# Two layers of linear attention and gated MLP: turning two more row tiles through DRAM instead of on TensorE

## The chip, the cores and the metric

The kernel runs on one core of a Trainium2 chip. A core has a matrix engine (TensorE, PE in the profile, with its weight loads as PEld), a vector engine (VectorE, DVE), a scalar engine (ScalarE, ACT), a general engine (GpSimd, POOL) and a sync engine (SyncE, SP), which here does nothing but issue DMA transfers. Each engine works through its own queue in order; they wait for each other through semaphores. SBUF is the memory on the core, PSUM the eight accumulation banks that TensorE writes, DRAM the memory off the core. The metric is the device time of one execution in microseconds, as the median of several runs.

## The reference

`x` has 2048 rows of 512 floats. Two layers follow each other with the same weights. In each, an attention block and a mixer block are added to `x`:

```python
x = x + A(layernorm(x))          # linear attention, 32 heads of 16
x = x + B(layernorm(x))          # gated MLP that mixes the rows

# A: phi(t) = where(t > 0, t + 1, exp(t)) + 1e-6
kv = einsum("bhsd,bhse->bhde", phi(k), v);  z = einsum("bhsd->bhd", phi(k))
o  = einsum("bhqd,bhde->bhqe", phi(q), kv) / (einsum("bhqd,bhd->bhq", phi(q), z) + 1e-6)
return o @ wo

# B: w_in is 512 x 1792, w_sp is 2048 x 2048
z  = gelu(x @ w_in);  z1 = z[:, :896];  z2 = layernorm(z[:, 896:])
return (z1 * (w_sp @ z2 + b_sp)) @ w_out
```

Everything is in float32 and has to stay that exact.

## The kernel before

**Numbers in two parts.** A float32 operand is split into a high part (a copy in the faster format float32r, made by ScalarE, line 224) and a low part (what is left over, made by VectorE, line 227, or by GpSimd, line 232). A product takes three matmuls: high by high, high by low, low by high (`mm3`, lines 238 to 240). So each operand of a matmul costs a ScalarE copy and a subtraction before TensorE can use it.

**Tiles and stages.** The rows are worked in 16 tiles of 128. For each layer L there are three stages. The first (`P1`) normalises the input, makes phi(q) and phi(k) and sums up k against the input. `transition` turns these sums into one 512 x 512 matrix `W2` and a vector. The second (`P2`) applies `W2` to each tile, adds the result to x, normalises to y, turns y so that features lie on the partitions, and multiplies y by `w_in`. The third (`P4`) mixes rows with `w_sp` and multiplies by `w_out`; its matmuls, lines 2076 to 2078, are most of the time.

**One step of the second stage.** `P2.run` (layer 0) and `P2.run2` (layer 1) are loops over steps s, with several tiles under way at a time. In step s:

- `c(s-1)`: twelve matmuls by `W2` into a PSUM bank; `c2` adds the bank to x (line 922) and takes the row statistics (lines 369 to 376, VectorE then GpSimd); `c3` stores x (line 928), normalises to y on ScalarE (line 382) and hands y to `Turn.store`.
- `a`, `a2` and `b`: multiply the queries of tiles s+3 and s+2 by their denominators (lines 867, 879 to 888), turn them, and split tile s for the next `c`.
- `d_high(s-2)` and `d_low(s-2)`: take up the turned y of tile s-2, with the high copy by ScalarE (line 224) and the low part by VectorE (line 227), written into a quarter of `xT`.
- `e(s-3)`: 24 matmuls of 448 columns for the half of `w_in` that is mixed later; `e2` is their gelu on ScalarE (line 1087), `e3` and `e4` the layer norm over it (line 382 again, 896 columns wide).
- `f`: twelve matmuls for the other half of `w_in`, on four tiles of y together; the first come in step 6, from when tiles 0 to 3 are in `xT`.

In layer 0, loads and adds of `w_sp` for the third stage go along in these steps (`sums.ask`, `sums.tick`; lines 1725, 1730), and pieces of `w_in` are loaded and split (`w1.piece`, `w1.fetch`). In layer 1 tiles from 4 on go through `epair` and `odd`, which the change does not touch.

**Two ways to turn a tile.** `Turn` (line 408) knows two. For a tile in its list `by_pe`, `get` runs four transposes of 128 x 128 on TensorE (line 394) into a PSUM bank. For another, `c3` normalises into another order of the columns, `store` writes the tile to DRAM by a transfer that SP issues (line 430), `load` reads it back in another layout (line 206), and `pre` turns its 32 x 32 blocks on VectorE (line 459). The turned tile goes to a PSUM bank in layer 0 for tiles below 13, and to the tile's own place in SBUF (`ZHome`) in layer 1. The queries are turned the same two ways with a list of their own: tiles 0 to 2 on TensorE, the others through DRAM (`qt`; in the DMA rows `qt<-pg` is a store and `pg<-qt` a load, and `yt` likewise for y).

**What sets the order.** All instructions are issued in the order of the program text; nothing is rescheduled. Where a DMA reads what another has written, SP waits for the landing and holds back all that it has to issue after that. In layer 0 a step asks SP for: the load of x for tile s+1; the store of x of tile s-1 and, if that tile goes through DRAM, its y store; the stores and loads of `sums.ask`; the query store of tile s+2; then, at the end of the step, the query load of tile s+2 (`qturn.load`), the y load of tile s-1 (`xturn.load`), and a piece of `w_in`. In layer 1 the query load comes at the head of the next step, so the y load of tile s-1 stands behind the query store of tile s+2.

SBUF is handed out in pages that go round (`pages`), and PSUM in eight banks likewise; whoever gets a page waits for the one who had it last.

Of the kernel before, what the change touches and what calls it, by code (L numbers as in the profile page):

```python
# [19 lines left out]
NT = S // P  # L20
# [103 lines left out]
QBANK = 13, 13  # L124
YBANK = 13
# [37 lines left out]
def mixer_kernel(ctx: ExitStack, tc: tile.TileContext, x_in, wqkv, wo_d, win1_d, win2_d, wsp_d, bsp_d, wout_d,  # L163
# [59 lines left out]
    def high(h, src):  # L223
        nc.scalar.activation(h, src, AF.Copy)  # L224

    def low(l, src, h):
        nc.vector.tensor_sub(l, src, h.bitcast(F32))  # L227

    def split(h, l, src, pool=False):
        high(h, src)  # L230
        if pool:
            nc.gpsimd.tensor_tensor(l, src, h.bitcast(F32), op=OP.subtract)
        else:
            low(l, src, h)
# [7 lines left out]
    class Weight:  # L242


        def __init__(self, slots, shape, pieces, turned=False):
            self.slots, self.shape, self.pieces, self.turned = slots, shape, pieces, turned
            self.h = self.l = None
            self.raw = deque()
            self.n_load = self.n_split = 0
# [40 lines left out]
    def w_in1():  # L290
        return Weight(bigs, [P, NF, 4, P], [win1_d[f] for f in range(NF)])
# [95 lines left out]
    def feats(ap, turned):  # L387

        return ap.rearrange("p (g c j) -> p c g j" if turned else "p (c g j) -> p c g j", g=4, c=4)
# [382 lines left out]
    def transition(p1, p2, sums):  # L772
        wv, wo = p1.wv, p1.wo
        zh, zl = pages.get(PAGE, F32R), pages.get(PAGE, F32R)
        za = p1.zacc
        nc.vector.tensor_scalar(za, za, NT * PHI_EPS, None, op0=OP.add)
        split(zh, zl, za, True)
        pages.put(za)
        p1.late()
        p1.wk.free()  # L780
        if p1.L == 0:
            sums.store2()
            sums.slots.close()
            sums.slots = pages
            sums.fetch()
        g = quads.get([P, 4, 512])
        for c in range(4):
            (high if c % 2 == 0 else nc.vector.tensor_copy)(g[:, c, :], p1.G[c])
            banks.put(p1.G[c])
        if p1.L == 0:  # L790
            sums.add2(0, 4)
        zb = banks.get(PAGE)
        nc.tensor.matmul(zb, ones, zh, start=True, stop=False)
        nc.tensor.matmul(zb, ones, zl, start=False, stop=True)
        pages.put(zh, zl)
        p2.zbc = pages.get(PAGE)
        nc.scalar.activation(feats(p2.zbc, True), feats(zb, False), AF.Copy)
        banks.put(zb)
        p2.a(0)
        p1.late_phi()  # L800
        if p2.win1 is not None:
            p2.win1.fetch()
            p2.win1.fetch()
        p2.zeps = small.tile([P, 32], F32, name="zeps", bufs=1)
        nc.vector.tensor_reduce(p2.zeps, p2.zbc.rearrange("p (h d) -> p h d", d=16), axis=mybir.AxisListType.X,
                                op=OP.add)
        nc.vector.tensor_scalar(p2.zeps, p2.zeps, PHI_EPS, PHI_EPS, op0=OP.mult, op1=OP.add)

        p2.a2_den(0)
        m = pages.get([P, 4, P])  # L810
        for q in range(4):
            b = banks.get([P, P])
            s = slice(q * P, (q + 1) * P)
            for c in range(4):
                nc.tensor.matmul(b, wv[:, c, s], g[:, c, s], start=c == 0, stop=c == 3)
            nc.vector.tensor_mul(m[:, q, :], b, mask)
            banks.put(b)
        quads.put(g, wv)
        p2.a2_mul(0)
        p2.a(1)  # L820
        p1.late()
        p2.a2_den(1)
        p2.W2 = (quads.get([P, 4, 512], F32R), quads.get([P, 4, 512], F32R))
        for q in range(4):
            b = banks.get(PAGE)
            nc.tensor.matmul(b, m[:, q, :], wo[:, q, :], start=True, stop=True)
            split(p2.W2[0][:, q, :], p2.W2[1][:, q, :], b)
            banks.put(b)
            if q == 1:
                p2.b(0)  # L830
        pages.put(m)
        quads.put(wo)
        p2.a(2)
        p1.late_phi()
        p2.a2_mul(1)
        p1.late()
        p2.a(3)
        p2.a2(2)
        p1.late_phi_a()


    class P2:
        def __init__(self, p1):
            self.L = L = p1.L
            self.p1 = p1
            self.win1, self.win2 = None if L else w_in1(), p1.win2
            self.ws = deque()
            self.wf = deque([] if not L else [w1parts[f] for f in list(range(NF)) * 2 + [0, 6, 1, 2, 6]]
                            + [w1sums[f, m] for m in range(2) for f in range(3)]
                            + [[t[:, 256:512] for t in w1parts[f + 3]] for f in range(3)])  # L850
            self.draw, self.S, self.fdone, self.qhome, self.zacc, self.meant = {}, {}, None, {}, {}, set()
            self.qturn, self.xturn = Turn(f"qt{L}", range(3), True, banked=range(QBANK[L])), Turn(f"yt{L}", (0, 1, 2, 3, NT - 1), home=ZHome, copy=bool(L), banked=() if L else range(YBANK))
            self.qp, self.qT, self.x, self.ms, self.xB, self.z, self.zms = {}, {}, {}, {}, {}, {}, {}
            self.fq = deque()
            self.fnext = []
            self.A, self.u, self.y = {}, {}, {}
# [484 lines left out]
        def run(self, sums):  # L1341
# [4 lines left out]
            for s in range(1, NT + 3):  # L1346
# [4 lines left out]
                if s < 5:  # L1351
                    self.c(s - 1)
                    self.b_high(s)
                    self.c2(s - 1)
                    self.p1.late_phi_b()
                    self.b_low(s)
                    if s >= 2:
                        self.d_high(s - 2)
                        self.d_low(s - 2)
                    self.p1.late()  # L1360
                    self.c3(s - 1)
                    sums.ask()
                    self.a2(s + 2)
                    self.p1.late_phi_a()
                    self.a(s + 3)
                    sums.tick(ask=False)
                else:
                    if s < NT:
                        self.b_high(s)
                    self.a2_den(s + 2)  # L1370
                    if s < NT:
                        self.b_low(s)
                    if s <= NT:
                        self.c(s - 1)
                        self.c2(s - 1)
                    if s == NT:
                        quads.put(*self.W2)
                        pages.put(self.zbc)
                    self.a2_mul(s + 2)
                    late = s - 2 in self.xturn.by_pe and s <= NT or AHEAD <= s <= NT  # L1380
                    if s in (NT, NT + 1):
                        self.e(s - 3)
                        self.e2(s - 3)
                    if late:
                        self.d_high(s - 2)
                        self.d_low(s - 2)
                    if s <= NT:
                        self.c3(s - 1)
                    self.a(s + 3)
                    if s <= NT + 1 and not late:  # L1390
                        self.d_high(s - 2)
                        self.d_low(s - 2)
# [106 lines left out]
        def run2(self):  # L1499
            late = self.p1  # L1500
            for s in range(1, NT + 3):
# [5 lines left out]
                if s < 5:  # L1507
# [2 lines left out]
                    self.c2(s - 1)  # L1510
                    late.late_phi_b()
                    self.b_low(s)
                    if s >= 2:
                        self.d_high(s - 2)
                        self.d_low(s - 2)
                    late.late()
# [1 line left out]
                    self.a2(s + 2)  # L1518
                    late.late_phi_a()
                    self.a(s + 3)  # L1520
                else:
                    def b():
                        if s < NT:
                            self.b_high(s)
# [1000 lines left out]
    p1 = P1(0)  # L2525
    p1.start()
    for L in range(2):
        p1.run(sums)
        p2 = P2(p1)
        p2.loadx(0)  # L2530
        p2.loadx(1)
        transition(p1, p2, sums)
        if L == 0:

            sums.store2()
            sums.tick()
        p2.p4 = p4 = P4(p2, sums)
        p2.run(sums)
        nxt = P1(1) if L == 0 else None
        p4.run(nxt)  # L2540
        p1 = nxt
# [31 lines left out]
```

## Time and profile before

| | |
|---|---|
| median of three runs | 1335.68 us (1335.37 to 1336.0) |
| the profiled execution | 1337.64 us, of which the span of its instructions is 1335.8 us |
| instructions | 19338, of them 6493 matmuls |
| TensorE clock granted | 1.00 over the span |
| data moved by DMA | 312.86 MB |
| line 793 of the transition starts, layer 0 and layer 1 | 129.70 us, 800.30 us |
| from the start of `e(0)` to the end of `e(3)`, layer 0 and layer 1 | 158.48 to 187.23 us, 829.56 to 858.31 us |

A row of a group reads: line, engine, operation, written tile <- read tiles, partitions x elements, count, then busy time and mean length. A row of the timeline reads: start in us, length in us, engine, line, operation, tiles, count, and in brackets how long the engine stood idle before it and what ended that. Matmuls overlap, so the time that a matmul takes from its neighbours is the distance between two starts and not its length. SPq rows are the issue of a transfer, not the transfer.

### The profile page before, as it was taken

How to read it: one execution, taken by the hardware profiler on the slowest of the kernel's cores; microseconds unless marked ns; L12 is line 12 of the kernel's file. 1: busy time of each engine (PE TensorE's matmuls, PEld its weight loads, DVE VectorE, ACT ScalarE, POOL GpSimd, SP SyncE). 2: the span in 40 equal slices, each digit the busy share in tenths (PEclk: the TensorE clock that was granted, in tenths of full speed). 3: DMA queues.
4: the chain of work that ended last, by engine and by line, in shares of the span. 5: the costliest groups of instructions: out<-in, count | busy, mean ns of one | idle time of the engine just before them, and what ended most of it. 6: DMA issues, size and time to landing. Idle time of an engine off the chain costs nothing.

```text
span 1335.8 us, 19338 instructions
## 1 busy us (share of the span) xinstructions
PE 1329.5 (100%) x6493; PEld 1132.0 (85%) x6493; DVE 1075.2 (80%) x1731; ACT 755.0 (57%) x1275; POOL 485.9 (36%) x632
## 2 busy tenths in 40 slices
PE   9999999999999999999999999999999999999998
PEld 7888888888888888889988878888888888888898
DVE  7679965768897889898867878678789988899885
ACT  5674543347743264445667755557588643666464
POOL 3765765533037400301424554554532022122021
PEclk9999999999999999999999999999999999999999
DMA  5898588987989896895987883678777876579344
GB/s 185 272 316 274 192 271 288 306 276 244 313 304 359 258 269 203 288 332 165 201 187 222 230 219 87 208 246 261 231 223 241 254 248 197 176 245 319 114 79 65
DMA packets 182532, 312.86 MB, mean 234 GB/s; under 512 B 15392, under 2 KB 56352, under 8 KB 182048
## 3 DMA queue, kind: packets, MB, share of 16 engines
q1 hardware_dynamic: 160672, 265.60, 59.6%
q0 software_dynamic: 21616, 45.88, 15.9%
q8 instruction: 51, 0.84, 0.3%
q14 instruction: 49, 0.40, 0.1%
q10 hardware_dynamic: 144, 0.13, 0.0%
HBM read 223.22 MB, written 113.51 MB: 252 GB/s over the span
## 4 chain that ended last, share of the span: by engine, by line
PE 87%; DVE 4%; DMA 4%; ACT 2%; POOL 2%; SPq 1%; issue 1%; POOLq 0%; DVEq 0%; ACTq 0%
PE bank L2076 12%; PE bank L2077 12%; PE bank L2078 12%; PE bank L240 10%; PE bank L238 10%; PE bank L239 10%; PE bank L2277 3%; PE bank L2278 3%; PE bank L2279 3%; PE bank L1173 1%; PE bank L1174 1%; PE bank L1172 1%; PE bank L1001 1%; PE bank L1003 1%; PE bank L1002 1%
## 5 line engine op out<-in xcount | busy, mean ns | idle before, releaser
L2076 PE MATMUL bank<-qd,pg 128*128 128x512 f32 x708 | 275.4, 389 | 0.0
L2077 PE MATMUL bank<-qd,pg 128*128 128x512 f32 x708 | 275.4, 389 | 0.0
L2078 PE MATMUL bank<-qd,pg 128*128 128x512 f32 x708 | 275.4, 389 | 0.0
L1829 ACT ACTIVATE qd<-qd 128x1024 fp32r<-128x1024 f32 x148 | 155.9, 1054 | 96.8 <-PE bank L2078 67.6
L1832 DVE TENSOR_TENSOR qd<-qd,qd 128x1024 fp32r<-128x1024 f32 x133 | 169.1, 1272 | 25.6 <-ACT qd L1829 25.4
L240 PE MATMUL bank<-qd,pg 128*128 128x512 f32 x448 | 174.8, 390 | 0.0
L2078 PEld LDWEIGHTS bank<-qd,pg 128*128 128x128 f32 x708 | 132.9, 188 | 27.7
L2076 PEld LDWEIGHTS bank<-qd,pg 128*128 128x128 f32 x708 | 132.9, 188 | 27.5
L2077 PEld LDWEIGHTS bank<-qd,pg 128*128 128x128 f32 x708 | 132.9, 188 | 27.3
L238 PE MATMUL bank<-qd,pg 128*128 128x512 f32 x264 | 103.2, 391 | 0.6 <-DVE pg L227 0.4
L239 PE MATMUL bank<-qd,pg 128*128 128x512 f32 x264 | 103.0, 390 | 0.0
L240 PEld LDWEIGHTS bank<-qd,pg 128*128 128x128 f32 x448 | 84.1, 188 | 18.4 <-DVE pg L227 0.9
L1730 POOL TENSOR_TENSOR pg<-pg,pg 128x512 f32<-128x512 f32 x48 | 71.9, 1498 | 64.7 <-DMA pg<-in_wsp_dram 60.4
L2117 POOL TENSOR_TENSOR bg<-bg,pg 128x512 f32<-128x512 f32 x28 | 52.1, 1863 | 115.4 <-ACT qd L1829 115.4
L373 POOL TENSOR_SCALAR rs<-mv 128x1 f32<-128x1 f32 x76 | 24.0, 315 | 165.8 <-DVE mv L371 159.7
L224 ACT ACTIVATE pg<-pg 128x512 fp32r<-128x512 f32 (+1 forms) x94 | 55.2, 597 | 51.0 <-DVE pg L1935 20.3
L2279 PE MATMUL bank<-wo,qd 128*128 128x256 f32 x288 | 81.5, 283 | 0.0
L2277 PE MATMUL bank<-wo,qd 128*128 128x256 f32 x276 | 78.1, 283 | 0.0
L2278 PE MATMUL bank<-wo,qd 128*128 128x256 f32 x276 | 78.0, 283 | 0.0
L227 DVE TENSOR_TENSOR pg<-pg,pg 128x512 fp32r<-128x512 f32 (+1 forms) x92 | 59.7, 657 | 5.7 <-ACT pg L224 5.4
L459 DVE STREAM_TRANSPOSE bank<-pg 128x512 f32<-128x512 f32 x58 | 41.6, 717 | 26.7 <-DMA pg<-yt 16.4
L238 PE MATMUL bank<-bg,qd 128*128 128x448 f32 x160 | 59.3, 371 | 0.1
(306 smaller groups left out, 3407.0 us busy)
## 6 DMA issues: line engine op xcount, KB each, us to landing
qd<-s SPq DMA_DIRECT2D x62, 512.0 KB, 5.0
qd<-hP SPq DMA_DIRECT2D x48, 512.0 KB, 5.0
qd<-in_wsp_dram SPq DMA_DIRECT2D x43, 512.0 KB, 4.9
pg<-z SPq DMA_DIRECT2D x56, 256.0 KB, 5.5
pg<-in_wsp_dram SPq DMA_DIRECT2D x52, 256.0 KB, 4.8
s<-pg SPq DMA_DIRECT2D x48, 256.0 KB, 4.3
z<-pg SPq DMA_DIRECT2D x40, 256.0 KB, 3.6
pg<-w POOLq DMA_DIRECT2D x38, 256.0 KB, 5.3
```

The source lines that it names most:

```text
L238: nc.tensor.matmul(out, ah, bh, start=start, stop=False)
L239: nc.tensor.matmul(out, ah, bl, start=False, stop=False)
L240: nc.tensor.matmul(out, al, bh, start=False, stop=stop)
L1730: nc.gpsimd.tensor_tensor(t, a, b, op=OP.add)
L1829: self.mark = nc.scalar.activation(w[:, 0], r, AF.Copy)
L1832: nc.vector.tensor_sub(w[:, 1], r, w[:, 0].bitcast(F32))
L2076: m(out, h[:, o], w[:, 0, j, :], start=start, stop=False, skip_group_check=True)
L2077: m(out, h[:, o], w[:, 1, j, :], start=False, stop=False, skip_group_check=True)
L2078: m(out, l[:, o], w[:, 0, j, :], start=False, stop=stop, skip_group_check=True)
L2277: m(out, A, x, start=start and f == 0, stop=False, skip_group_check=True)
L2278: m(out, A, y, start=False, stop=False, skip_group_check=True)
L2279: m(out, B, x, start=False, stop=stop and f == 2, skip_group_check=True)
```

## The change

Three places change.

1. In `transition`, the low part of the sum of phi(k) (`zl`) is made by GpSimd in layer 0, as it was, and by VectorE in layer 1. In VectorE's queue it stands ahead of the copies of `G` (line 788), in TensorE's it is read by line 794.
2. `xturn`'s list `by_pe` loses tiles 2 and 3, in both layers. These two tiles of y are now normalised into the other order, stored, loaded and turned on VectorE, like tiles 4 to 14.
3. In the first steps, `d` of tile s-2 stood behind `b_low` and ahead of `c3`. For tiles 0 and 1 it stays there. For tile 2 it moves to the end of step 4, behind `c3`, `a2`, `a` and, in layer 0, `sums.tick`. For tile 3, in step 5, no line moves, but the list decides there too: a tile that is not in `by_pe` is taken up behind `c3` instead of ahead of it (`late` in layer 0, `ahead` in layer 1).

```diff
@@ transition
-        split(zh, zl, za, True)
+        split(zh, zl, za, p1.L == 0)
@@ P2.__init__
-            ... self.xturn = Turn(f"yt{L}", (0, 1, 2, 3, NT - 1), home=ZHome, copy=bool(L), banked=() if L else range(YBANK))
+            ... self.xturn = Turn(f"yt{L}", (0, 1, NT - 1), home=ZHome, copy=bool(L), banked=() if L else range(YBANK))
@@ P2.run, steps 1 to 4
-                    if s >= 2:
+                    if 2 <= s < 4:
                         self.d_high(s - 2)
                         self.d_low(s - 2)
                     self.p1.late()
...
                     self.a(s + 3)
                     sums.tick(ask=False)
+                    if s == 4:
+                        self.d_high(2)
+                        self.d_low(2)
@@ P2.run2, steps 1 to 4
-                    if s >= 2:
+                    if 2 <= s < 4:
                         self.d_high(s - 2)
                         self.d_low(s - 2)
                     late.late()
...
                     self.a(s + 3)
+                    if s == 4:
+                        self.d_high(2)
+                        self.d_low(2)
```

More of the change, by code (lines that the diff above doesn't have):

```diff
@@ L851, in __init__ @@
             self.draw, self.S, self.fdone, self.qhome, self.zacc, self.meant = {}, {}, None, {}, {}, set()
-            self.qturn, self.xturn = Turn(f"qt{L}", range(3), True, banked=range(QBANK[L])), Turn(f"yt{L}", (0, 1, 2, 3, NT - 1), home=ZHome, copy=bool(L), banked=() if L else range(YBANK))
+            self.qturn, self.xturn = Turn(f"qt{L}", range(3), True, banked=range(QBANK[L])), Turn(f"yt{L}", (0, 1, NT - 1), home=ZHome, copy=bool(L), banked=() if L else range(YBANK))
             self.qp, self.qT, self.x, self.ms, self.xB, self.z, self.zms = {}, {}, {}, {}, {}, {}, {}
```

## The prediction

> **What bounds the kernel now.** I read the page first, then what TensorE (PE) waited for, then the timeline of each engine around the two stretches where tiles 2 and 3 of y are handled, layer 0 at 163 to 189 us and layer 1 at 834 to 859 us.
>
> ```profile
> span 1335.8 us, 19338 instructions
> ...
> PE 1329.5 (100%) x6493; PEld 1132.0 (85%) x6493; DVE 1075.2 (80%) x1731; ACT 755.0 (57%) x1275; POOL 485.9 (36%) x632
> ```
>
> ```profile
> PE bank L623 <- DVE ones_f L189: 1.0, 1, 1.0
> ```
>
> PE is busy in 1329.5 of 1335.8 us, and its longest single wait is 1.0 us, at the very start. So PE's issue order is the time: whatever leaves PE is gained in full, and whatever PE has to wait for in the new order is lost in full, since no later gap gives it back. The sum is made against the profiled execution (1337.64 us, its span 1335.8 and 1.8 around it); the timed median is 1335.68, 1.96 lower, and I carry the difference that I work out over to the median.
>
> **The change part by part.** I write d(i) for taking up tile i of y (turn, high copy on ScalarE, low part on VectorE), e(i) for its gate matmuls, which need d(i), and c(i) for the projection that makes tile i.
>
> *What PE loses.* Here is d(2) in layer 0, the turn between c(3) and e(1):
>
> ```profile
> 166.28 0.60 PE L394 MATMUL bank<-ident,pg 128*128 128x128 f32 x4
> ...
> 166.92 0.37 PE L239 MATMUL bank<-bg,qd 128*128 128x448 f32 x1
> 167.12 0.36 PE L240 MATMUL bank<-bg,qd 128*128 128x448 f32 x1
> ```
>
> From the first transpose to the second matmul of e(1) it is 0.64 us; one matmul of e takes a slot of 0.20 (167.12 - 166.92), so four transposes hold PE for 0.44. Two tiles in two layers: 4 x 0.44 = 1.76 us gone. The row shows why length misleads: 0.60 for four that overlap. [...] The trace has slots of 0.11, and I use those.
>
> *What comes instead in layer 0.* The tile is normalised in the other layout (L382, 0.82 us for either), stored, loaded back and turned on VectorE. The stores and loads go through SP's queue, in program order. Step 3 issues: x store of tile 2 (L928), then, new, the y store of tile 2; sums and spatial-weight transfers; the q store of tile 5 (L430); at the step's end the q load of tile 5, and right behind it, new, the y load of tile 2.
>
> ```profile
> 163.95 0.38 SPq L928 DMA_DIRECT2D x<-pg  x1
> ...
> 168.17 0.41 SPq L430 DMA_DIRECT2D qt<-pg  x1
> 172.87 0.33 SPq L206 DMA_DIRECT2D pg<-qt  x1
> 173.25 0.42 SPq L206 DMA_DIRECT2D pg<-in_win_dram  x1
> ...
> 176.54 1.22 SPq L430 DMA_DIRECT2D qt<-pg  x1
> 181.50 0.32 SPq L206 DMA_DIRECT2D pg<-qt  x1
> ```
>
> The q load stands at the head of the queue from 168.6 until its own store has landed, 172.87. The y load of tile 2 can't pass it: it is issued where L206's win load is now, 173.25, and later by what the new y store takes in front of it. The seven transfers from the x store of 163.95 to the q store were through at 172.87, so one costs at most 1.3; I take half of that, 0.65, and 173.9 for the issue.
>
> ```profile
>   DVE bank L459: 16.4, 9
> ...
> DMA to landing us min/median/max: 2.6/3.3/6.6
> ```
>
> That is the answer for the y transfers of layer 0: the loads of later tiles land 2.6 us after issue at best, 3.3 in the middle, and VectorE has already waited 16.4 us for nine of them. I take 2.9, between the first two, since the queue has just been waited out: landed at 176.8. Bounds: 173.25 + 2.6 = 175.9 and 174.5 + 6.6 = 181.1.
>
> ```profile
> 171.58 0.39 PE L238 MATMUL bank<-qd,pg 128*128 128x512 f32 x1
> ...
> 174.32 0.60 PE L394 MATMUL bank<-ident,pg 128*128 128x128 f32 x4
> ...
> 179.62 0.40 PE L238 MATMUL bank<-qd,z_q 128*128 128x512 f32 x1
> ```
>
> ```profile
> 172.65 1.33 DVE L888 SCALAR_TENSOR_TENSOR pg<-z_q,den 128x512 f32<-128x512 f32 x1
> ...
> 176.54 0.69 DVE L459 STREAM_TRANSPOSE bank<-pg 128x512 f32<-128x512 f32 x1
> ...
> 178.55 0.69 DVE L227 TENSOR_TENSOR pg<-bank,z_q 128x512 fp32r<-128x512 f32 x1 [0.16 <-DMA x<-pg]
> ...
> 181.27 0.69 DVE L227 TENSOR_TENSOR qd<-bank,qd 128x512 fp32r<-128x512 f32 x1
> ```
>
> ```profile
> 162.68 0.82 ACT L382 ACTIVATE pg<-pg,nb,rs 128x512 f32<-128x512 f32 x1 [1.69 <-POOL nb L376]
> ...
> 173.65 1.12 ACT L382 ACTIVATE z_z<-z_z,nb,rs 128x896 f32<-128x896 f32 x1
> ...
> 177.26 0.60 ACT L224 ACTIVATE z_q<-bank 128x512 fp32r<-128x512 f32 x1 [1.12 <-DVE bank L459]
> ...
> 182.49 0.82 ACT L382 ACTIVATE pg<-pg,nb,rs 128x512 f32<-128x512 f32 x1 [4.14 <-POOL nb L376]
> ```
>
> First wait, e(2). VectorE's step 4 ends with L888 (172.65 + 1.33 = 174.0); then, new, d(2) sits there until 176.8. Turn 0.69, high copy 0.60, low part 0.69: the high part is there at 178.2, the low part at 178.9. e(2)'s third matmul is the first to read the low part, two slots of 0.20 behind its first, so e(2) starts as if at 178.5. PE gets there when c(4) is done: 174.32 less the transposes of d(2) = 173.9. The wait is 4.6 us (3.7 with the early bound, 8.9 with the late one).
>
> Second wait, e(3). ScalarE's queue holds the high copy of d(2) ahead of e(0)'s normalise (now 173.65) and e(1)'s two gelus, so these start at about 178.1 and the b part of tile 5 follows as it does now: turn 2.9 after that normalise (176.54 - 173.65), low part 2.0 after the turn (178.55), so 182.9 to 183.6. c(5) is reached at 178.5 + 4.86 = 183.4 (e is 174.76 to 179.62 now): no wait. The normalise of tile 4 comes 3.9 after that low part starts (182.49 - 178.55), at 186.8; d(3) is no longer ahead of it but behind it, so its high copy is done at about 188.2 and its low part at 188.9; the y load of tile 3, behind the q load of 181.50 (and 2.0 later for three new transfers of 0.65), is issued at 183.8, lands near 186.7 and is turned by 187.4, just in time. e(3) starts as if at 188.5; PE has done c(5) (2.74 long) at 186.1. Wait 2.4 (1.3 if the normalise is not late, 3.5 with one slow transfer). In step 6, e(3) and two f tiles (twelve matmuls each, as c) give VectorE and ScalarE 4.86 + 2 x 2.74 = 10.3 us to catch up, and nothing of this is passed on.
>
> Layer 0: +4.6 + 2.4 - 0.88 = **+6.1 us**.
>
> *Layer 1.* Here the q load is issued a step later in the order and the y load of tile 2 stands right behind the q store of tile 5:
>
> ```profile
> 835.17 0.37 SPq L430 DMA_DIRECT2D qt<-pg  x1
> ...
> 839.00 0.32 SPq L206 DMA_DIRECT2D pg<-qt  x1
> ```
>
> ```profile
> 841.61 1.69 DVE L888 SCALAR_TENSOR_TENSOR pg<-z_q,den 128x512 f32<-128x512 f32 x1
> ...
> 846.47 0.69 DVE L227 TENSOR_TENSOR pg<-bank,z_q 128x512 fp32r<-128x512 f32 x1 [1.35 <-ACT z_q L224]
> ...
> 858.05 1.09 DVE L459 STREAM_TRANSPOSE z_y<-pg 128x512 f32<-128x512 f32 x1
> ```
>
> ```profile
> 842.25 1.12 ACT L382 ACTIVATE z_z<-z_z,acc 128x896 f32<-128x896 f32 x1
> ...
> 850.40 0.82 ACT L382 ACTIVATE pg<-pg,nb,rs 128x512 f32<-128x512 f32 x1 [3.48 <-POOL nb L376]
> ```
>
> ```profile
> 850.71 0.40 PE L238 MATMUL bank<-qd,z_q 128*128 128x512 f32 x1
> ...
> 853.45 0.36 PE L238 MATMUL bank<-bg,qd 128*128 128x448 f32 x1
> ```
>
> The y store stands ahead of 835.17 and the load waits for it some 3 to 4 us (the q store took 3.8), so it lands by about 842. VectorE frees at 842.7 (L888's end less the 0.6 of the low part that is gone from before it), or near 841.7 if L888 doesn't take 1.69 there. The turn into SBUF is 1.09, the high copy 0.60: e(0)'s normalise (842.25) moves to between 843.4 and 844.4, by 1.1 to 2.1. e(2), at 850.71 - 4.86 - 0.88 = 845.0, has its low part at 845.1 at the latest, before its third matmul. The b part of tile 5 (846.47) moves to 848.6 at most, c(5) is at 849.8: covered. The normalise of tile 4 (850.40) moves to 851.5 to 852.5; high copy and low part of d(3) behind it end 2.05 later, so e(3) starts as if at 853.1 to 854.2, against 853.45 - 0.88 = 852.6. Wait 0.5 to 1.6, I take 1.0. Layer 1: 1.0 - 0.88 = **+0.1**.
>
> *The low part in layer 1's transition.*
>
> ```profile
> 798.78 1.27 DVE L788 COPY qd<-bank 128x512 f32<-128x512 f32 x2
> ...
> 799.61 1.29 POOL L232 TENSOR_TENSOR pg<-pg,pg 128x512 fp32r<-128x512 f32 x1 [1.70 <-ACT pg L224]
> ...
> 800.30 0.39 PE L793 MATMUL bank<-pg,ones 128*128 128x512 f32 x1
> 800.95 0.50 PE L794 MATMUL bank<-pg,ones 128*128 128x512 f32 x1 [0.26 <-POOL pg L232]
> 801.28 1.95 PE L815 MATMUL bank<-qd,qd 128*128 128x128 f32 x16
> ```
>
> PE waits for POOL's low part: L794 could start a slot of 0.23 behind L793, at 800.53, and starts 0.4 later. On VectorE the part takes 0.69 from 799.6, so it is there at 800.3 and the 0.4 is saved. But the two G copies now stand behind it and end at 801.5 instead of 800.1, and L815, which could begin at 800.9, reads them: if each matmul needs its own quarter, the last copy is just in time; if the first one needs all four, it starts at 801.5, 0.2 later than now. Between -0.4 and +0.2; I take **-0.2**.
>
> Sum: 6.1 + 0.1 - 0.2 = **+6.0 us**, 1335.68 + 6.0 = **1341.7 us**. With the low ends (3.7 + 1.3 - 0.88, 0.5 - 0.88, -0.4) it is +3.3; with the high ends (8.9 + 3.5 - 0.88, 1.6 - 0.88, +0.2) +12.4.
>
> **The rivals.**
>
> *No wait at all.* If both tiles were back before PE needs them, only the 1.76 and the 0.4 count: 1335.68 - 2.2 = 1333.5. It speaks for it that later tiles take this way without holding PE up. Against it: their steps hold f tiles besides, while step 5 lasts 8.0 (171.58 to 179.62), and it decides only if the y load is issued by 169.3, 4.6 us earlier, ahead of the q load that holds the queue. Chance 0.05.
>
> *Only a short wait.* One of the two waits in layer 0 falls out, because the load is taken out of its turn or d(3) finds ScalarE free before the normalise: 6.0 - 4.6 = +1.4 or 6.0 - 2.4 = +3.6, so 1337.1 or 1339.3. Chance 0.12.
>
> *The clock falls as well.* A gap of 4.6 us would be several times the longest so far.
>
> ```profile
> 2.35 3.41 PE L630 MATMUL bank<-pg,ones 128*128 128x512 f32 x8
> ```
>
> At the start, after idling, PE issued eight matmuls of 512 columns in 3.41 us, 0.43 each; in c(4) twelve take 2.74, 0.23 each. If a gap brings that pace back for 3.4 us, half of it is lost: +1.7, so 1343.4. No gap in this trace is long enough to tell. [...] Chance 0.18.
>
> *More waits.* The pages go round in another order and a reused one may be held by a store (L227 at 178.55 waits 0.16 for the x store's page now); with a wait as long as the late bound of the first, 1335.68 + 12.4 = 1348.1. Chance 0.05.
>
> **How the numbers follow.** The forecast has the remaining 0.60. The range takes the low and high ends of the sum without the rarest: 1337.2 to 1346.2. It holds the forecast but for its outermost ends, the fall of the clock, and the upper half of the short-wait case. A measurement of this kernel can tell about 0.2% (2.7 us): faster would be under 1333.0, no change up to 1338.4. The no-wait case is within 0.2%, so faster has 0.03; and so is the nearer half of the short-wait case, with a little of the forecast's low end: 0.13; slower 0.84.
>
> **What would show it.** PE should show waits before the first matmuls of e(2) and e(3) in layer 0 (L238 with 448 columns) of about 4.6 and 2.4 us, released by VectorE's L227 or ScalarE's L224, and one near 1 us in layer 1. SP should issue the y load of tile 2 between 173 and 174.5, behind a q load; VectorE's L459 should wait for it from 174 on. There should be 16 fewer transposes on L394. The wait of L794 on POOL should be gone. I am wrong if that y load is issued before 170, or if e(2) in layer 0 starts within 1 us of c(4)'s end.

## The result, and the profile after

The changed kernel takes 1344.07 us (median of six runs, 1343.53 to 1348.9), the kernel before beside it 1335.84 (six runs, 1334.76 to 1338.6). The ratio is 1.0065 with a 95% interval of 1.0048 to 1.0081: slower by 6 to 11 us. Predicted was 1341.7, in a range of 1337.2 to 1346.2. Further down, a ratio is turned into microseconds by taking 1336 as the time before.

The profiled execution after took 1348.9 us (clock 0.996 over the span). The head of its page, and what TensorE waited for (line of the waiting instruction, releaser, then microseconds in total, times, the longest):

```profile
span 1347.0 us, 19318 instructions
PE 1333.0 (99%) x6477; PEld 1133.8 (84%) x6477; DVE 1074.7 (80%) x1736; ACT 754.4 (56%) x1275; POOL 484.1 (36%) x631
```

```profile
PE bank L238 <- ACT qd L224: 6.0, 2, 4.4
PE bank L238 <- ACT z_h L224: 2.8, 1, 2.8
```

There are 16 matmuls fewer, as there should be. The two waits on the high copies of `qd` are e(2) and e(3) of layer 0. The wait on `z_h` comes and goes between executions, as shown below. The row of L794 waiting on GpSimd is gone.

Now layer 0 around tiles 2 and 3. First SP's issues (start, length of the issue):

```profile
172.21 0.33 SPq L206 DMA_DIRECT2D pg<-qt  x1
172.59 0.42 SPq L206 DMA_DIRECT2D pg<-yt  x1
...
177.66 0.60 SPq L430 DMA_DIRECT2D qt<-pg  x1
182.80 0.32 SPq L206 DMA_DIRECT2D pg<-qt  x1
183.21 0.38 SPq L206 DMA_DIRECT2D pg<-yt  x1
```

Both y loads go out directly behind a q load, and each q load has waited for its own store: the one of 177.66 holds the queue until 182.80. VectorE then sits before the turn of each tile (in brackets the idle time and what ended it), and ScalarE before the high copy:

```profile
176.43 0.73 DVE L459 STREAM_TRANSPOSE bank<-pg 128x512 f32<-128x512 f32 x1 [3.05 <-DMA pg<-yt]
...
187.47 0.73 DVE L459 STREAM_TRANSPOSE bank<-pg 128x512 f32<-128x512 f32 x1 [2.38 <-DMA pg<-yt]
```

```profile
177.19 0.60 ACT L224 ACTIVATE qd<-bank 128x512 fp32r<-128x512 f32 x1 [4.12 <-DVE bank L459]
...
188.23 0.60 ACT L224 ACTIVATE qd<-bank 128x512 fp32r<-128x512 f32 x1 [1.19 <-DVE bank L459]
```

And TensorE, from the last matmul of c(4) into e(2), and from the last of c(5) into e(3):

```profile
173.08 0.39 PE L240 MATMUL bank<-qd,pg 128*128 128x512 f32 x1
177.84 0.74 PE L238 MATMUL bank<-bg,qd 128*128 128x448 f32 x1 [4.37 <-ACT qd L224]
178.38 0.57 PE L239 MATMUL bank<-bg,qd 128*128 128x448 f32 x1
178.75 0.57 PE L240 MATMUL bank<-bg,qd 128*128 128x448 f32 x1
...
180.99 0.39 PE L240 MATMUL bank<-bg,qd 128*128 128x448 f32 x1
181.22 0.37 PE L238 MATMUL bank<-bg,qd 128*128 128x448 f32 x1
...
186.85 0.39 PE L240 MATMUL bank<-qd,pg 128*128 128x512 f32 x1
188.88 0.47 PE L238 MATMUL bank<-bg,qd 128*128 128x448 f32 x1 [1.64 <-ACT qd L224]
```

Start to start, 173.08 to 177.84 is 4.76 where 0.23 would do: 4.5 us lost. But the loss does not end there. The next matmuls start 0.37 apart (178.38 to 178.75) where one of 448 columns takes 0.20: nine of them, from 177.84 to 181.22, take 3.38 us instead of 1.84, so 1.5 more are lost. TensorE came back from the gap at about half its pace: the granted clock is 0.50 from 177.63 to 181.04 and 1.00 on both sides of that. The second gap costs 1.8 us (188.88 less 186.85 less 0.23), and 0.2 more where the third matmul waits for the low part. In the kernel before there was no gap ahead of e(3):

```profile
182.14 0.39 PE L240 MATMUL bank<-qd,pg 128*128 128x512 f32 x1
182.36 0.36 PE L238 MATMUL bank<-bg,qd 128*128 128x448 f32 x1
```

Layer 1's e(3) starts 0.46 behind the last matmul of c(5), where 0.23 is a slot, and the transition no longer waits:

```profile
862.99 0.39 PE L240 MATMUL bank<-qd,pg 128*128 128x512 f32 x1
863.45 0.47 PE L238 MATMUL bank<-bg,qd 128*128 128x448 f32 x1
```

```profile
811.41 0.39 PE L793 MATMUL bank<-pg,ones 128*128 128x512 f32 x1
811.64 0.40 PE L794 MATMUL bank<-pg,ones 128*128 128x512 f32 x1
811.88 3.73 PE L815 MATMUL bank<-qd,qd 128*128 128x128 f32 x32
```

From L793 to L815 it was 0.98 before (801.28 - 800.30) and is 0.47 now.

### The profile page after: what moved, and what is told of

It reads as the page before. It is cut to its first block, busy times and chain, and to the rows that moved or that the text cites. A ratio compares the mean times of both kernels' runs of the same rounds, so it can differ in the third digit from the quotient of the medians.

```text
span 1347.0 us, 19318 instructions
## 1 busy us (share of the span) xinstructions
PE 1333.0 (99%) x6477; PEld 1133.8 (84%) x6477; DVE 1074.7 (80%) x1736; ACT 754.4 (56%) x1275; POOL 484.1 (36%) x631
## 4 chain that ended last, share of the span: by engine, by line
PE 91%; DVE 3%; DMA 2%; ACT 2%; issue 1%; POOL 1%; SPq 0%; POOLq 0%; ACTq 0%; DVEq 0%
PE bank L2083 12%; PE bank L2084 12%; PE bank L2082 12%; PE bank L240 11%; PE bank L238 11%; PE bank L239 11%; PE bank L2283 3%; PE bank L2284 3%; PE bank L2285 3%; PE bank L1174 1%; PE bank L1173 1%; PE bank L1172 1%; DMA pg<-xt 1%; PE bank L1001 1%; PE bank L1003 1%; PE bank L1002 1%
```

## The experiments

The theory: all of the loss is in layer 0 and is made of e(2)'s and e(3)'s waits for a y load that stands behind a q load on SP's queue. The rivals: layer 1 or the transition carries part of it; the order on SP's queue does not matter, because the transfer itself or VectorE's place for it is late; the clock, not the wait, is what costs.

**The change in layer 0 alone, and in layer 1 alone.** The list of tiles, the order of `d` and the transition, each by layer:

```diff
# layer 0 alone
-   Turn(f"yt{L}", (0, 1, NT - 1), ...)
+   Turn(f"yt{L}", (0, 1, 2, 3, NT - 1) if L else (0, 1, NT - 1), ...)
    run2 and transition as before the change
# layer 1 alone
+   Turn(f"yt{L}", (0, 1, 2, 3, NT - 1) if L == 0 else (0, 1, NT - 1), ...)
    run as before the change
```

> The change in layer 0 alone: tiles 2 and 3 through DRAM and tile 2 at the end of step 4 there, layer 1 and its transition as before. Theory (two waits of TensorE in layer 0, for e(2) and e(3), carry the loss, and layer 1 gains a little): 6.5 to 8 us slower than before, with waits of about 4.4 and 2 us on L238 before e(2) and e(3) and slow matmuls after the first. Rival (a good part of the loss comes with layer 1, for example the wait of 2.8 us near 786 us that the profile after shows): 5 us slower or less.

> The change in layer 1 alone, with the low part of its transition on VectorE; layer 0 as before. Theory: 8 transposes at 0.11 and the wait of L794 go (0.88 and 0.42), a wait of about 0.45 before e(3) comes, so 0.6 to 1.1 us faster than before. Rival (layer 1 carries part of the loss): 1 to 2 us slower.

Layer 0 alone: 1343.59 us, ratio 1.0053 (1.004 to 1.0066), so +7.1 us (5.3 to 8.8). Layer 1 alone: 1336.94, ratio 1.0007 (0.9996 to 1.0019), between -0.5 and +2.5. The place is layer 0. In its profile e(3), expected to wait about 2 us, waits only some 0.6 with the low part, and e(2) waits as in the changed kernel:

```profile
177.86 0.47 PE L238 MATMUL bank<-bg,qd 128*128 128x448 f32 x1 [4.18 <-ACT qd L224]
```

The gain expected of layer 1 alone is not to be seen; a gain of more than 0.5 us is excluded. Its e(3) starts 0.71 behind c(5), a wait of 0.5:

```profile
855.47 0.39 PE L240 MATMUL bank<-qd,pg 128*128 128x512 f32 x1
856.18 0.47 PE L238 MATMUL bank<-bg,qd 128*128 128x448 f32 x1 [0.33 <-ACT qd L224]
```

The profile of layer 1 alone also bears on the wait on `z_h`, of which it has its own:

```profile
PE bank L238 <- ACT z_h L224: 2.9, 1, 2.9
```

It is in layer 1's first stage, near 783 us, ahead of everything that this kernel changes, and the profiled execution of before has no wait over 0.5 us there. So it comes and goes by execution; no trace here shows it in the kernel before itself. In the profile after, this wait and the slow matmuls behind it (granted clock 0.50 from 788.61 to 795.44) take some 5.6 us; that execution lay 4.8 above its median. The changed kernel was run again:

> The changed kernel once more, on the chip of these runs. Theory: 7 to 8.5 us slower than before, with waits of 4.4 us before e(2) and 0.5 to 2 us before e(3) in layer 0 and slow matmuls behind the first; a wait of some 3 us late in layer 1's first stage, which the profile after showed and the one of before did not, comes and goes from run to run and is no part of the change. Rival: that wait is there again and makes a part of the 8 us.

It gave 1344.15 us, ratio 1.0058 (1.0045 to 1.007), and a profiled execution of 1343.89, where e(2) and e(3) of layer 0 read:

```profile
173.62 0.39 PE L240 MATMUL bank<-qd,pg 128*128 128x512 f32 x1
177.67 0.47 PE L238 MATMUL bank<-bg,qd 128*128 128x448 f32 x1 [3.66 <-ACT qd L224]
...
187.09 0.39 PE L240 MATMUL bank<-qd,pg 128*128 128x512 f32 x1
188.33 0.47 PE L238 MATMUL bank<-bg,qd 128*128 128x448 f32 x1 [0.85 <-ACT qd L224]
```

Without the `z_h` wait, this execution is 6.25 us above the profiled one of before (1343.89 - 1337.64). Its terms are taken up below.

**The y load ahead of the q load.** In steps 3 and 4 of layer 0 the two loads change places:

```diff
+               if s in (3, 4):
+                   self.xturn.load(s - 1)
                self.qturn.load(s + 2)
-               self.xturn.load(s - 1)
+               if s not in (3, 4):
+                   self.xturn.load(s - 1)
```

> As the changed kernel, but in layer 0 the y loads of tiles 2 and 3 are issued ahead of the query loads of steps 3 and 4 instead of behind them. Theory (the wait for e(2) is mostly the y load standing behind a query load that holds SP's queue until its own store has landed): the load of tile 2 is issued near 168.5 instead of 172.6, e(2) waits 1.5 to 2 us instead of 4.5, no slow matmuls follow, e(3) waits 1 to 2.5; 3 to 4 us slower than before, so 4 to 5 us faster than the changed kernel. Rival (VectorE's and ScalarE's order binds, not the queue): e(2) still waits 3.5 us or more and the time stays within 1 us of the changed kernel's.

1340.83 us, ratio 1.004 (1.0027 to 1.0054): +5.3 us, 2.4 to 3.3 less than the changed kernel by the ratios and the medians, where 4 to 5 less had been expected.

```profile
169.39 0.45 SPq L206 DMA_DIRECT2D pg<-yt  x1
174.33 0.32 SPq L206 DMA_DIRECT2D pg<-qt  x1
```

```profile
174.93 0.73 DVE L459 STREAM_TRANSPOSE bank<-pg 128x512 f32<-128x512 f32 x1 [1.58 <-DMA pg<-yt]
```

```profile
176.34 0.68 PE L238 MATMUL bank<-bg,qd 128*128 128x448 f32 x1 [2.28 <-ACT qd L224]
176.82 0.57 PE L239 MATMUL bank<-bg,qd 128*128 128x448 f32 x1
```

The queue's order is a third to a half of the first wait: with the load out 3.2 us earlier (169.39 against 172.59; 173.35 in the second profile), e(2)'s loss falls from 4.5 (3.8 in the second profile) to 2.4 (176.34 - 173.67 - 0.23, c(4)'s last matmul starting at 173.67). Half of the head start or more is eaten by the transfer, which now needs 5.5 us until VectorE has the tile (169.39 to 174.93) instead of 3.8 or 2.9. In this trace the three loads of `w_sp` and the query store issued ahead of it land at 172.22, 172.89, 173.55 and 174.31 and the y load at 174.91, in the order of their issue. So the query load's wait is not all: the four transfers ahead came through first. And two expectations fell: the matmuls behind the shorter gap are slow all the same, 0.37 apart, and e(3), expected to wait 1 to 2.5 us, starts 0.4 behind its slot (185.41 to 186.07), so that here the 1.5 us of slow matmuls are not hidden in a second wait. (This execution also has the wait on `z_h` and took 1345.16 us.)

**The gap filled with work.** Twenty matmuls of 448 columns whose result is overwritten, ahead of e(2) in layer 0:

```diff
+               if self.L == 0 and i == 2 and j == 0:
+                   for _ in range(20):
+                       nc.tensor.matmul(b, self.W2[0][:, 0, 0:P], self.W2[0][:, 0, 0:HF], start=True, stop=True)
```

> As the changed kernel, with 20 matmuls of 448 columns whose result is overwritten put in front of e(2) in layer 0; they take about 4.1 us and keep TensorE busy while it would wait. Both theories: the matmuls of e(2) keep the fast slot of 0.20 us. Theory (the slow matmuls lengthen the kernel): 1.2 to 1.6 us faster than the changed kernel. Rival (the next wait, for tile 3's load, does not move with TensorE, so e(3) starts when it did): within 0.4 us of the changed kernel, and the wait before e(3) grows from 2.0 to about 3.5 us.

1345.17 us, ratio 1.0062 (1.0048 to 1.0075): no better than the changed kernel, as the rival had it. The profiled execution took 1348.60, 3.4 above the median:

```profile
173.61 4.22 PE L1073 MATMUL bank<-qd 128*128 128x448 f32 x20
178.78 0.48 PE L238 MATMUL bank<-bg,qd 128*128 128x448 f32 x1 [0.94 <-ACT qd L224]
...
189.95 0.74 PE L238 MATMUL bank<-bg,qd 128*128 128x448 f32 x1 [2.98 <-ACT qd L224]
```

The work did keep e(2) fast, but e(3) now waits 3 us and it is there that the slow matmuls come, and they go on twice as long, from 189.95 to 196.1. Tile 3 is not back sooner because TensorE works faster: its load is issued when SP's queue gets to it (in this execution behind a q load of 184.63). So what is saved at e(2) is waited for at e(3). What the slow matmuls alone cost, this run can't tell, as it has longer ones of its own.

**One tile alone.** Tile 3 alone through DRAM in layer 0, and tile 2 alone, with everything else as before:

```diff
# tile 3 alone
+   Turn(f"yt{L}", (0, 1, 2, 3, NT - 1) if L else (0, 1, 2, NT - 1), ...)
# tile 2 alone, with its d at the end of step 4
+   Turn(f"yt{L}", (0, 1, 2, 3, NT - 1) if L else (0, 1, 3, NT - 1), ...)
```

> In layer 0 tile 3 alone goes through DRAM; tile 2 stays on TensorE in its old place, layer 1 and its transition are as before. Theory (the load of a tile is ready at a time that SP's queue sets, whatever TensorE does; in the changed kernel the first wait hides most of the second): the y load of tile 3 is issued near 182.7 behind a query load and lands near 186 to 187, e(3) would be reached at 181.9 and waits 5 to 6.5 us; 5 to 8 us slower than before, almost what both tiles cost together. Rival (each tile adds its own price, and tile 3's is the 0.6 to 2 us that e(3) waits in the changed kernel): 0 to 2 us slower.

> Layer 0 with tile 2 alone turned through DRAM and taken up at the end of step 4; tile 3, layer 1 and the transition as before. The wait before e(2) must come as in the changed kernel, 3.8 to 4.5 us, and, being longer than 3.9 us or near it, one window at half clock behind it (eight or nine matmuls of 448 columns at 0.37 instead of 0.20, 1.5 us); tile 3 is turned on TensorE, so e(3) should start without a wait of over 0.5. Theory: 4.2 + 0.2 + 1.5 less the 0.44 of the transposes, +5.5 us (4.5 to 6.5). The costs of tile 2 alone (5.5) and of tile 3 alone (measured +6.1) would then add up to 11.6, where the two together cost 6.9 to 8: they overlap. Rival (the clock costs nothing here, only the wait counts): +3.5 to +4.2. Rival (costs add up): both together minus tile 3 alone, +1 to +2.

Tile 3 alone: 1342.54 us, ratio 1.0038 (1.0025 to 1.0052), +5.1 us (3.3 to 6.9). Tile 2 alone: 1341.74, ratio 1.0044 (1.0032 to 1.0056), +5.9 us (4.3 to 7.5). Together that would be 11.0; both tiles in layer 0 cost 7.1. (The 6.1 in the second expectation is tile 3's difference of the medians; its 3.9 us is an estimate from the bursts further down, where all 15 gaps from 3.35 us up were followed by slow matmuls.) Tile 3's e(3), and tile 2's e(2):

```profile
186.07 0.56 PE L238 MATMUL bank<-bg,qd 128*128 128x448 f32 x1 [4.26 <-ACT qd L224]
```

```profile
174.49 0.66 PE L394 MATMUL bank<-ident,pg 128*128 128x128 f32 x4 [0.35 <-ACT pg L382]
178.37 0.69 PE L238 MATMUL bank<-bg,qd 128*128 128x448 f32 x1 [3.22 <-ACT qd L224]
```

In both, nine matmuls or so behind the wait are slow. e(3) of the first starts at 186.07, with tile 2 no trouble at all; in the changed kernel at 188.88 or 188.33. Its wait is 4.4 us (186.07 less 181.42, where c(5)'s last matmul starts, less 0.23) where 5 to 6.5 was expected, as the load went out at 181.74 and not near 182.7; in the changed kernel it goes out at 183.21 or 183.94, so tile 2's transfers do move the queue by some 2 us. Tile 3 isn't there before 186 on this queue, and the 6 us that e(2) loses ahead of it hide most of its wait. That is why the two do not add up. The second kernel's wait is 3.2 where 3.8 to 4.5 was expected: the transposes of tile 3 fall into the gap. It also shows the price of the slow matmuls by themselves: its e(3) doesn't wait and starts 9.29 us behind e(2) (187.66 less 178.37), where it was 7.69 before (182.36 less 174.67), 1.6 more with little but slow matmuls between.

**Tile 3 taken up earlier in layer 1, and the transition alone.**

```diff
# run2, with the change in layer 1 alone
-                   ahead = s - 2 in self.xturn.by_pe
+                   ahead = s - 2 in self.xturn.by_pe or s == 5
# the kernel before, transition
-       split(zh, zl, za, True)
+       split(zh, zl, za, p1.L == 0)
```

> The change in layer 1 alone, as before, and in its step 5 tile 3 is taken up ahead of the normalise of tile 4 again. Theory (e(3) of layer 1 waits because its high copy stands behind that normalise on ScalarE): the wait of 0.5 to 0.7 us on L238 before e(3) in layer 1 goes; 1.0 to 1.4 us faster than before. Rival (tile 3's own transfer is late): the wait stays, 0.3 to 0.7 us faster.

> The transition's low part on VectorE in layer 1, nothing else changed. Theory: the wait of line 794 on GpSimd (0.2 to 0.4 us) is gone, line 815 starts no later behind line 794 than a slot, -0.4 us; too little for the timed runs to show. Rival (the copies of G behind the new instruction hold line 815 up): 0 to +0.2. The trace of lines 793 to 815 decides, not the time.

The first gave 1335.73 us, ratio 0.9997 (0.9984 to 1.0009), the second 1336.39, ratio 1.0001 (0.9989 to 1.0014): neither can be told from the kernel before, and the 1.0 to 1.4 us expected of the first are not shown. So the version made of all that gains by its trace is not shown to beat it. The traces do tell something. With tile 3 taken up ahead, e(3)'s first matmul comes without a wait, a slot behind c(5), but the third one now waits 0.28 for the low part:

```profile
852.14 0.39 PE L240 MATMUL bank<-qd,pg 128*128 128x512 f32 x1
852.37 0.36 PE L238 MATMUL bank<-bg,qd 128*128 128x448 f32 x1
852.57 0.37 PE L239 MATMUL bank<-bg,qd 128*128 128x448 f32 x1
853.05 0.47 PE L240 MATMUL bank<-bg,qd 128*128 128x448 f32 x1
```

In the transition alone L793, L794 and L815 start at 801.05, 801.28 and 801.52, each a slot behind the one before it, as in the profile after: the copies of `G` do not hold L815 up.

**How long a gap slows TensorE.** A kernel that does nothing but bursts of 70 to 79 matmuls of 512 columns, with gaps that copies on ScalarE make longer step by step, ten gap lengths four times over, in one run:

> Not the reference's computation: the input is copied to the output, and beside that 40 bursts of 70 to 79 matmuls of 512 columns follow each other, with a gap between two bursts that grows in ten steps from about 1 to about 6 us through a chain of copies, four times over. Theory from the traces so far (gaps of 1.8 us left the matmuls fast, gaps of 2.4 and more did not): the first matmuls after a gap are slow, 0.43 apart instead of 0.23, from a gap of about 2 to 2.4 us on. [...]

The gaps came out at 1.25 to 4.37 us. Rows of four bursts' beginnings, with how many matmuls fell into how much time, and the gap ahead in brackets:

```profile
73.03 3.25 PE L186 MATMUL b<-m,r 128*128 128x512 f32 x13 [1.99 <-DVE m L190]
```

```profile
492.33 4.84 PE L186 MATMUL b<-m,r 128*128 128x512 f32 x13 [1.99 <-DVE m L190]
```

```profile
555.87 4.61 PE L186 MATMUL b<-m,r 128*128 128x512 f32 x19 [3.01 <-DVE m L190]
```

```profile
339.99 7.31 PE L186 MATMUL b<-m,r 128*128 128x512 f32 x19 [3.01 <-DVE m L190]
```

The same gap of 1.99 us is followed by thirteen matmuls in 3.25 us or in 4.84, the same gap of 3.01 by nineteen in 4.61 or 7.31. Over the 39 gaps: none of the 8 of up to 1.65 us is followed by slow matmuls, 9 of the 16 between 1.99 and 3.01 are, and all 15 from 3.35 up. A slow stretch costs about 1.5 us, or some 2.6 when it goes on twice as long. So no one length divides these gaps, and the expected one, about 2 to 2.4 us, was not found. More shows in this trace's record of the granted clock (0.935 over the span): behind the gaps it is at half in 24 stretches, each 3.413 us long or twice that, and all of them lie on one grid of 3.413 us that runs through the whole trace. On that grid, the gaps with at most 1.86 us of idle time in any one of its windows were here never followed by a slow stretch, those with 1.99 or more always. The stretch was twice as long where the idle time went on for 0.79 us or more in the next window, and not where it went on for 0.44 or less. The two stretches at half clock in the profile after, 3.41 and 6.83 us long, also fit such a grid: their starts lie 610.98 us apart (788.61 - 177.63), 179 times 3.4133. In the second profile of the changed kernel (clock 0.95 from 172 to 180, 0.89 from 180 to 192) 1.84 us in one window was enough, so the edge between 1.86 and 1.99 does not hold to better than some 0.1 us.

Carried over to the kernel, as an estimate from these numbers: a gap on TensorE of under 1.8 us would have no such price, one above 4.0 (twice 1.99, so that one window gets 1.99 of it) would pay it wherever it lies, and between them its place on the grid, which the program does not set, would decide. The kernel before has no gap over 1.0 us; the ones here, from 2.3 to 4.4, were all followed by slow matmuls.

## Why the prediction was right, and where its sizes were off

**What bounds the kernel.** Right: what TensorE has to wait for in layer 0 is in the time, and nothing gives it back. Counted from line 793 of layer 0, e(3) there starts at 52.66 us in the profile before and at 58.67 in the second one after, 6.0 later, and the execution ends 6.3 later. The rivals without a wait or with a short one would have needed the y load of tile 2 before 170; even with that, in the kernel with the load ahead, 5.3 us are lost.

**Transposes.** 16 matmuls gone; no trace speaks against 1.76 us. (The formats apart: in the trace of before, line 815's 16 products in plain float32, of 128 columns each, take 3.49 us, 133.66 - 130.17, so 0.22 for one, where 448 columns in float32r take 0.20.)

**The first wait.** Right in place, cause and size. The y load was said to go out at 173.9 behind the q load, to land 2.9 later at 176.8, and to make e(2) wait 4.6. It went out at 172.59 (173.35 in the second profile), was there at 176.43 (176.26), and e(2) lost 4.5 (3.8). The 0.65 for the new y store in front was not needed, as SP was waiting for the q store's landing anyway, so in the first profile the load left a little earlier than the 173 to 174.5 that was given as the sign; the landing took 3.8 there and 2.9 in the second. The late bound rests on a misreading: the 6.6 us come from a view that counts stores with loads; in the trace of before the y loads of layer 0 alone land 2.6 to 3.7 us after their issue, so the 8.9 and the high end of the sum had no such load behind them.

**The second wait.** Right that there is one, too large: 2.4 predicted, 2.0 and 1.2 measured, with the low part. The turned tile came at 188.2 instead of 187.4 (187.7 in the second profile), so e(3) started at 188.88 (188.33) where 188.5 was worked out. But TensorE was late as well: it had finished c(5) at 187.1 and not at 186.1, because the clock had fallen. The load of tile 3, not the normalise of tile 4, was the last to arrive; the prediction had them nearly level. Its low end of 1.3 does not follow from its own rows either: a tile turned by 187.4 and a high copy of 0.60 hold e(3) until 188.0, a wait of 1.9.

**The clock.** This is the step that was mis-sized. It stood as a rival of chance 0.18 that would cost 1.7 us on top and had no place in the sum, and it happened in every profile of a kernel with the wait in layer 0: 1.5 us, and a stretch twice as long with the gap filled. With tile 2 alone, where no second wait follows, it is in the time. With both tiles it falls into the second wait, since the load of tile 3 sets the start of e(3): the two waits were to cost 7.0 (4.6 and 2.4), and in the second profile the waits and the clock together cost 6.7 (4.0, 1.2 and 1.5). That the missing term and the waits taken too long nearly cancel is luck.

**Layer 1.** A wait of 1.0 was predicted before e(3), against 0.88 gained. The traces have 0.45 (after) and 0.7 (second profile), with the low part. Net it is a gain of 0.2 to 0.4 that no timing could show. In the trace of layer 1 alone nothing of it is left: e(3) there starts 0.86 us sooner behind line 793 than before, the transition's part included, but the third stage starts at the same distance (209.80 us against 209.78), as 0.3 go at e(3)'s low part and 0.6 in small waits near 980.

**The transition.** -0.2 was taken between -0.4 and +0.2; by the rows above it is -0.5 (0.98 to 0.47). L815 isn't held up, as the low end had it.

**The sum.** In the second profile of the changed kernel: 4.0 at e(2) with the low part, 1.5 for the clock, 1.2 at e(3), 0.7 in layer 1, less 1.76 and 0.5, makes +5.1; the two profiled executions differ by 6.25, and the missing 1.1 is in small waits elsewhere (0.9 of it from 970 to 986 us, on lines 1001 to 1172; the traces of layer 0 alone and of layer 1 alone lose 0.5 and 0.6 there, that of tile 2 alone nothing, and what starts them is open). The forecast was +6.0. So the sum fits the profiles; the median moved by 8.2, or by 7.7 against the 17 executions of before that ran beside the second run (1344.15 less 1336.46). The step that failed there is "I carry the difference that I work out over to the median": the profiled execution of before lay 1.96 above its median, while the changed kernel's second one lay 0.3 below. What cost the profiled execution of before these 2 us is not settled, as there is only one trace of it. Nor is it settled what starts the wait on `z_h` near 785 us in some executions.

## What to carry to other kernels

A transfer that is issued behind another one's wait on the same queue is as late as that wait (in the profile after the y loads of layer 0 went out at 172.59 and 183.21, right behind q loads of 172.21 and 182.80 that had waited for their stores): before moving work from a busy engine to a round trip through memory, find the slot in which its load will be issued and compare it with the time at which the result is due. Costs of two late tiles are not to be added (5.1 and 5.9 us alone, 7.1 together): the first wait hid the second, and filling the first uncovered it. A gap on TensorE of 2 us or more can bring another 1.5 us of slow matmuls behind it (9 of 16 gaps from 1.99 to 3.01 us in the bursts did, and all 15 longer ones); whether they lengthen the kernel depends on whether a later wait hides them (with tile 2 alone 1.6 us stayed in the time, with both tiles they fell into the second wait).

## What had not been expected of the hardware

The clock fell after gaps as short as 2.28 us in the kernel and 1.99 in the bursts, and the length of a gap did not decide it: the same gap of 3.01 us cost nothing twice and about 1.4 and 2.7 us the other two times, by where it lay on the grid of 3.413 us in the record of the granted clock. For the y load issued first, taking its place ahead bought only 1.5 of 3.2 us at VectorE (174.93 against 176.43): its transfer took 5.5 us instead of 3.8 and landed behind the four issued ahead of it, at 172.22 to 174.31.
